# Attention with normalized queries and keys: half of the first shifted line of each batch made by GpSimd, squares made by VectorE

## The chip, the core and the metric

The kernel runs on one core of one Trainium2 chip. The metric is the device time of one execution in microseconds. A core has five engines that run side by side, each through its own list in its own order: TensorE (PE in the profile, its weight loads PEld), VectorE (DVE), ScalarE (ACT), GpSimd (POOL) and SyncE (SP, which issues DMAs). They wait for one another by semaphores.

## The reference

Attention of 32 heads, 2048 queries and keys, head size 20, all bf16. Queries and keys are divided by their norm, the logits are scaled by a number per head.

```python
qn = q / (jnp.sqrt((q * q).sum(axis=-1, keepdims=True)) + eps)
kn = k / (jnp.sqrt((k * k).sum(axis=-1, keepdims=True)) + eps)
logits = jnp.einsum('bhqd,bhkd->bhqk', qn, kn) * t[None, :, None, None]
attn = softmax(logits, axis=-1)
return jnp.einsum('bhqk,bhkd->bhqd', attn, v)
```

## The kernel before

**Tiling.** Four heads make a head group; there are eight. A head group has four query blocks of 512 queries (32 in all, numbered `sb`). A unit is 128 keys of one head against the 512 queries of a block: 64 units in a block. For each unit TensorE makes the logits in PSUM (128 keys by 512 queries), an engine turns them into exponentials in SBUF, and TensorE multiplies these with the values and adds into psO, one PSUM bank which belongs to one query block at a time. A column of ones beside the values gives the denominators.

**Two ways to the exponential.** In most units ScalarE does it, in waves of three and two units in turn (psA to pA, line 822; 14 waves fit in pA). The others, quota `ND_SB` = 18 of the 64 in a block and 20 in the last head group, go through VectorE: line 284 (`p1_op`, the conversion) multiplies a tile of psD and adds a constant so that the result, written as int16 and read as fp16, is about the exponential; `SHIFTS[0]` is part of the constant. Three more copies of it, shifted by the other numbers of `SHIFTS` (line 293, `chain_ops`: an int16 add), are multiplied with the values too, so that the errors of the four average out. One of the four copies is used a second time with values halved (`vhalf`): `COEF` says which, five products for each unit. Four units make a batch (`DB`): four conversions of 128x512, then three shift lines over the whole batch, 128x2048. Buffers dI, dS1, dS2, dS3 hold five batches (`NBD`); the batch number modulo five is the buffer number `bb`.

**Normalization.** For the next head group, while the current one is computed, `prep_ops` squares q and k (line 212 on GpSimd in pieces of 128x160, or line 216 on VectorE as 128x640), sums the squares (line 219), takes the inverse root on VectorE (lines 236 to 251) and scales (line 264, on GpSimd in pieces of two rows, `NM_ROWS`). DMAs transpose the result into qT and kT. The first head group does it all on VectorE. At the end of each query block VectorE transposes psO (line 315) and takes reciprocals (line 317), and GpSimd multiplies (line 319).

**Order.** All orders are fixed when the program is built. `make_plan` runs a small planner with assumed costs, step by step in time, and each engine gets its list from it. VectorE takes, of what is ready, the lowest priority number: 0 the end of a query block, 1 conversions (`PRIO1`), 1.5 normalization (`PRIO`), 2 shift lines. GpSimd's work lies in a list of its own with the same numbers (`step_pool`, line 956): it may start while VectorE is idle, or in the first 0.1 of an operation that the planner counts as free of the shared port (`port` false: the conversion, the transpose, sums, reciprocals; line 179). If it starts beside such an operation, it gets a wait on the VectorE operation before that one (lines 971 and 972), so that it starts with it on the chip too. VectorE operations with `port` true do not start in the planner while GpSimd is busy (line 941); on the chip no semaphore holds them. TensorE's list is made by `step_pe0`: logits when a PSUM buffer is free, else products with the values (`pv_round`, line 656), and only of the query block that owns psO; holes are filled with products of zeros (line 503).

Of the kernel before, what the change touches and what calls it, by code (L numbers as in the profile page):

```python
# [9 lines left out]
I32 = mybir.dt.int32  # L10
I16 = mybir.dt.int16
# [2 lines left out]
AXIS_X = mybir.AxisListType.X  # L14

LOG2E = 1.4426950408889634
SHIFTS = (382, 860, 565, 123)
COEF = ((1,), (1,), (1,), (1, .5))
LOG2K = 2.685380
NPV = sum(len(c) for c in COEF)  # L20

# [31 lines left out]
POOL2 = .0022  # L53
SQ_ROWS = 1
NM_ROWS = 2


class Op:
# [45 lines left out]
def bass_standalone__qk_norm__prompt_kernel(  # L104
# [7 lines left out]
    B, H, S, D = q.shape  # L112
# [5 lines left out]
    QW = 512  # L118

    with ExitStack() as es:  # L120
        sbuf = lambda name, shape, dt: es.enter_context(nc.sbuf_tensor(name, shape, dt))
# [19 lines left out]
        dI = sbuf("dI", [128, NBD, DB * QW], I16)  # L141
        dS = [dI] + [sbuf(f"dS{i}", [128, NBD, DB * QW], I16) for i in range(1, len(SHIFTS))]
        zt = sbuf("zt", [128, QW], BF16)
        iot = sbuf("iot", [128, 128], F32)
        idn = sbuf("idn", [128, 128], BF16)
        nr0 = sbuf("nr0", [128, 2, NH, 4], F32)
# [27 lines left out]
        def dve(name, n, rate, emit, reads, writes, ncols_fix=0.0, info=None):  # L174
            c = n * rate
            o = Op("DVE", name, emit, reads, writes, cost=0.069 + c + ncols_fix,
                   lat=0.135 + c + ncols_fix, info=info)

            o.port = name not in ("P1", "cp", "drain", "red", "inv", "rec")
            return o  # L180
# [7 lines left out]
        def prep_ops(hg, r0, r1, a0=0, a1=2, pool=False):  # L188
# [8 lines left out]
            for c0 in range(r0, r1, 4 * 2 // na):  # L197
                nn = min(4 * 2 // na, r1 - c0)
                bs = n_sq[0] % 2
                n_sq[0] += 1  # L200
                src = qk[b][:, a0:a1, :, c0:c0 + nn, :]
                w_ = na * NH * nn * D
                sq = sqs[bs][:, 0:w_]
                x3 = src.rearrange("p a h r d -> p (a h) (r d)")
                s3 = sq.rearrange("p (h x) -> p h x", h=na * NH)
                s4 = sq.rearrange("p (h r d) -> p h r d", h=na * NH, r=nn)
                o4 = ssum[b][:, a0:a1, :, c0:c0 + nn].rearrange("p a h r -> p (a h) r")
                if pool:
                    for c in range(0, nn, SQ_ROWS):
                        k0, k1 = c * D, min(c + SQ_ROWS, nn) * D  # L210
                        ops.append(pool_op("sq", na * NH * (k1 - k0), True,
                                           lambda e, o=s3[:, :, k0:k1], x=x3[:, :, k0:k1]: e.tensor_tensor(o, x, x, ALU.mult),  # L212
                                           kq, [("sqs", bs, c)]))
                else:
                    ops.append(dve("sq", w_, R2,
                                   lambda e, o=s3, x=x3: e.tensor_tensor(o, x, x, ALU.mult),
                                   kq, [("sqs", bs)] + [("sqs", bs, c) for c in range(R)]))
                ops.append(dve("red", w_, R1,
                               lambda e, o=o4, x=s4: e.tensor_reduce(o, x, AXIS_X, ALU.add),  # L219
                               [("sqs", bs)] + [("sqs", bs, c) for c in range(R)], [SS]))  # L220
# [59 lines left out]
        def p1_op(pb, bb, j):  # L280
# [3 lines left out]
                       lambda e: e.tensor_scalar(dst, psD[:, pb * QW:(pb + 1) * QW], 1024.0 * LOG2E, 15360.0 - 1024.0 * LOG2K + SHIFTS[0], ALU.mult, ALU.add),  # L284
                       [("psD", pb)], [("dI", bb, j)])

        def chain_ops(bb, nu):


            W = nu * QW  # L290
            kI = [("dI", bb, j) for j in range(nu)]
            return [dve(f"S{i}", W, R4,
                        lambda e, i=i: e.tensor_single_scalar(dS[i][:, bb, 0:W], dI[:, bb, 0:W],  # L293
                                                              float(SHIFTS[i] - SHIFTS[0]), ALU.add),
                        kI, [(f"dS{i}", bb, j) for j in range(nu)]) for i in range(1, len(SHIFTS))]

        def half_op(hg):
            b = hg % 2
# [78 lines left out]
        def make_plan(share):  # L377
# [57 lines left out]
            def finish(op, start, cost, lat):  # L435
                op.start, op.done = start, start + lat
                P.put(op)
# [9 lines left out]
            def zeros(i, after=()):  # L447
# [8 lines left out]
            finish(o, 0.05, o.cost, o.lat)  # L456
            o = P.link(Op("DVE", "z", lambda e: e.memset(act_scr[:, :], 1.0), [], ["scr"], 0.1, 0.15))
            finish(o, 0.3, o.cost, o.lat)
            o = P.link(dve("idn", 128, R1, lambda e: e.tensor_single_scalar(idn[:, :], iot[:, :], 0.0, ALU.is_equal),
                           ["iot"], ["idn"]))  # L460
            finish(o, 1.0, o.cost, o.lat)
# [403 lines left out]
            def step_qkd(used, with_a):  # L865
                nonlocal d_sb, issued_d
                while d_sb < NSB and d_left[d_sb] == 0:
                    d_sb += 1
                if d_sb >= NSB or d_sb > a_sb + 1:
                    return False  # L870
                if pe_mid:
                    return False
                rds = P.readers.get(("psD", issued_d % 2), [])
                if not all(r.done is not None and r.done + SEML <= now for r in rds):
                    return False
                if P.last_w.get(("psD", issued_d % 2)) is not None and not rds:
                    return False
                done_a = sum(quota[:a_sb]) + quota[a_sb] * (1 - a_left[a_sb] / aq[a_sb]) if a_sb < NSB else 1e9
                if issued_d > done_a + LEAD:
                    return False  # L880
                nb = len(batches)
                if batches and len(batches[-1]["u"]) < DB:
                    nb -= 1
                else:
                    if nb >= NBD:
                        old = [(nm, nb % NBD, j) for j in range(DB) for nm in ["dI"] + [f"dS{i}" for i in range(1, len(SHIFTS))]]
                        if any(x[3] in old for x in pending_pv):
                            return False
                if d_sb not in pool:
                    pool[d_sb] = units_of(d_sb)  # L890
                save = {hh: list(x) for hh, x in pool[d_sb].items()}
                us = take(d_sb, used, 1, "D")
                if not us or not keys_ready(us) or (with_a and us[0][1] in used):
                    pool[d_sb] = save
                    return False
                u = us[0]
                d_left[d_sb] -= 1
                pv_all[d_sb][u[1]] += NPV - 1
                pb = issued_d % 2
                issued_d += 1  # L900
                if not batches or len(batches[-1]["u"]) == DB:
                    batches.append({"u": [], "p": []})
                bt = batches[-1]
                bi = len(batches) - 1
                bb, j = bi % NBD, len(bt["u"])
                bt["u"].append(u)
                pe_group("QKD", [qk_mm(u, psD[:, pb * QW:(pb + 1) * QW])], "qk", qk_keys(u), [("psD", pb)], [u[1]])
                bt["p"].append(p1_op(pb, bb, j))
                want_dve(bt["p"][-1], PRIO1)
                total_left = sum(d_left)  # L910
                if len(bt["u"]) == DB or total_left == 0:
                    nu = len(bt["u"])
                    ch = chain_ops(bb, nu)
                    for o in ch:
                        want_dve(o, 2 + 0.001 * bi)
                    for j2, uu in enumerate(bt["u"]):
                        for i, cs in enumerate(COEF):
                            o, nm = (ch[i - 1], f"dS{i}") if i else (bt["p"][j2], "dI")
                            x = dS[i][:, bb, j2 * QW:(j2 + 1) * QW].bitcast(F16)
                            for c in cs:  # L920
                                pending_pv.append((o, uu, x, (nm, bb, j2), c != 1))
                return True
# [33 lines left out]
            def step_pool():  # L956

                on = P.order["DVE"]
                busy = free_["DVE"] > now
                if busy and (on[-1].port or now > on[-1].start + 0.1):  # L960
                    return False
                best = None
                for x in pool_todo:
                    ra_ = ready_at(x[2])
                    if ra_ is not None and ra_ <= now and (best is None or x[:2] < best[:2]):
                        best = x
                if best is None:
                    return False
                pool_todo.remove(best)
                o = best[2]  # L970
                if busy and len(on) > 1 and on[-2] not in o.deps:
                    o.deps.append(on[-2])
                finish(o, now, o.cost, o.lat)
                free_["POOL"] = now + o.cost
                return True
# [198 lines left out]
```

## Time and profile before

| | |
|---|---|
| runs, median (lowest to highest) | 720.33 us (720.0 to 721.35) |
| the profiled execution | 721.53 us |
| its span (first to last instruction) | 719.7 us |
| granted TensorE clock, mean | 0.994 |
| instructions | 17473 |
| ScalarE exponentials (L822) | 597 |
| VectorE conversions (L284), shift lines (L293) | 556, 417 |
| GpSimd squares (L212), scalings (L264), last products (L319) | 112, 112, 31 |

A row of the groups gives the line of the kernel, the engine, what is written and read with shapes and count, then the busy time in us, the mean of one in ns, and the idle time of the engine just before them with who ended it. A row of the timeline gives start, duration, engine, line and count; the same operations in a row are merged. Matmul ends are modelled, and a full TensorE may be full of zero products.

The chain of work that ended last runs by turns over TensorE (45%), ScalarE (37%) and VectorE (15%).

### The profile page before, as it was taken

To read this page: it belongs to the slowest core of one execution; us is meant where nothing else is said; L and a number is where in the kernel's file an instruction comes from. 1 tells how busy PE (TensorE), PEld (TensorE's weight loads), DVE (VectorE), ACT (ScalarE), POOL (GpSimd) and SP (SyncE) were. 2 spreads that over 40 slices of the span, in tenths; PEclk is the share of its full clock that TensorE was granted. 3 is DMA by queue.
4 is the path that set the end of the run, shared out by engine and by line. 5 is a ranking of instruction groups with operands and counts; after the bars stand their busy time and mean duration, and the time that the engine had idled before them with its cause. 6 is when DMAs were issued, how large, how long until landed. Compare 5 with 4: busy or idle time off the path is not lost.

```text
span 719.7 us, 17473 instructions
## 1 busy us (share of the span) xinstructions
PE 697.3 (97%) x7572; PEld 244.4 (34%) x7572; DVE 679.6 (94%) x1218; ACT 691.1 (96%) x605; POOL 135.1 (19%) x268
## 2 busy tenths in 40 slices
PE   7999999999999999999999999999999999999996
PEld 4433333433333333333333332342333433323332
DVE  6799959999999999999999999999999999999992
ACT  5999999979999999999999999999999989999996
POOL 2031234031040310311203130122201221000000
PEclk8999999999999999999999999999999999999999
DMA  5510133013030220300421022301203002000000
GB/s 60 83 7 2 30 68 38 2 30 68 1 39 1 31 66 2 37 2 1 82 29 26 1 45 53 38 2 31 67 1 38 1 18 44 2 19 7 1 6 14
DMA packets 113859, 19.68 MB, mean 27 GB/s; under 512 B 103024, under 2 KB 113776, under 8 KB 113776
## 3 DMA queue, kind: packets, MB, share of 16 engines
q1 hardware_dynamic: 112960, 18.37, 16.7%
q8 instruction: 61, 1.00, 0.6%
q10 hardware_dynamic: 816, 0.12, 0.1%
q14 instruction: 22, 0.18, 0.1%
HBM read 7.87 MB, written 2.62 MB: 15 GB/s over the span
## 4 chain that ended last, share of the span: by engine, by line
PE 45%; ACT 37%; DVE 15%; issue 0%; DMA 0%; ACTq 0%; SPq 0%
ACT pA L822 37%; PE psO L656 23%; PE psA L634 13%; DVE dS L293 7%; DVE dI L284 7%; PE psD L634 5%; PE psO L503 3%; DVE accT L315 1%; DVE ssum L219 1%; DMA tb<-in_t_dram 0%; ACTq L1121 0%; DVE vhalf L300 0%; DVE rsb L247 0%; DVE rsa L245 0%; DVE rsa L244 0%
## 5 line engine op out<-in xcount | busy, mean ns | idle before, releaser
L822 ACT ACTIVATE pA<-psA 128x1536 bf16<-128x1536 f32 x597 | 686.9, 1268 | 16.1 <-PE psD L634 9.9
L284 DVE TENSOR_SCALAR dI<-psD 128x512 int16<-128x512 f32 x556 | 355.5, 676 | 17.9 <-PE psD L634 15.5
L293 DVE TENSOR_SCALAR dS<-dI 128x2048 int16<-128x2048 int16 x417 | 276.0, 691 | 0.0
L634 PE MATMUL psA<-qT,kT 32*128 32x512 bf16 x1742 | 256.6, 384 | 7.7 <-ACT pA L822 4.5
L656 PE MATMUL psO<-dS,vaug 128*32 128x512 f16 x1668 | 222.5, 384 | 0.6 <-DVE dS L293 0.4
L656 PE MATMUL psO<-pA,vaug 128*32 128x512 bf16 x1492 | 221.0, 384 | 0.1
L634 PE MATMUL psD<-qT,kT 32*128 32x512 bf16 x556 | 178.9, 381 | 1.1 <-DVE dI L284 0.7
L634 PEld LDWEIGHTS psA<-qT,kT 32*128 32x128 bf16 x1742 | 62.9, 91 | 167.8 <-ACT pA L822 115.0
L656 PE MATMUL psO<-dI,vaug 128*32 128x512 f16 x556 | 115.3, 384 | 3.4 <-DVE accT L315 3.2
L656 PE MATMUL psO<-dS,vhalf 128*32 128x512 f16 x556 | 101.0, 382 | 0.3 <-DVE dS L293 0.2
L503 PE MATMUL psO<-zt 128*128 128x128 bf16 x976 | 101.0, 225 | 0.0
L319 POOL TENSOR_TENSOR ost<-accT,rec 128x320 bf16<-128x320 f32 x31 | 24.1, 777 | 354.2 <-DVE dS L293 246.4
L656 PEld LDWEIGHTS psO<-dS,vaug 128*32 128x32 bf16 x1668 | 60.1, 94 | 70.7 <-issue 33.8
L503 PEld LDWEIGHTS psO<-zt 128*128 128x128 bf16 x976 | 60.8, 99 | 66.2 <-issue 63.7
L656 PEld LDWEIGHTS psO<-pA,vaug 128*32 128x32 bf16 x1492 | 60.4, 94 | 56.1 <-issue 37.8
L212 POOL TENSOR_TENSOR sqs<-qk 128x160 bf16<-128x160 bf16 x112 | 50.8, 453 | 82.2 <-DVE dI L284 39.6
L634 PEld LDWEIGHTS psD<-qT,kT 32*128 32x128 bf16 x556 | 40.5, 91 | 50.1 <-DVE dI L284 29.0
L264 POOL TENSOR_TENSOR kpad<-qk,rn 128x160 bf16<-128x160 bf16 x56 | 26.3, 469 | 85.9 <-DVE dI L284 46.7
L656 PEld LDWEIGHTS psO<-dI,vaug 128*32 128x32 bf16 x556 | 30.0, 94 | 25.9 <-DVE accT L315 12.3
L264 POOL TENSOR_TENSOR qpad<-qk,rn 128x160 bf16<-128x160 bf16 x56 | 28.7, 517 | 42.6 <-DVE dS L293 36.0
L656 PEld LDWEIGHTS psO<-dS,vhalf 128*32 128x32 bf16 x556 | 26.3, 95 | 25.4 <-issue 13.5
L315 DVE STREAM_TRANSPOSE accT<-psO 128x512 f32<-128x512 f32 x32 | 22.6, 706 | 9.9 <-PE psO L656 9.9
(54 smaller groups left out, 101.3 us busy)
## 6 DMA issues: line engine op xcount, KB each, us to landing
vaug<-in_v_dram SPq DMA_DIRECT2D x32, 80.0 KB, 4.0
qk<-in_k_dram SPq DMA_DIRECT2D x7, 320.0 KB, 4.1
qk<-in_q_dram SPq DMA_DIRECT2D x7, 320.0 KB, 4.2
out_dram<-ost SPq DMA_DIRECT2D x28, 80.0 KB, 1.9
out_dram<-ost SPq DMA_DIRECT2D x14, 20.0 KB, 1.6
qk<-in_k_dram SPq DMA_DIRECT2D x1, 240.0 KB, 3.8
qk<-in_q_dram SPq DMA_DIRECT2D x1, 240.0 KB, 4.3
kT<-kpad SPq DMA_TRANSPOSE x8, 4.3
```

The source lines that it names most:

```text
L212: lambda e, o=s3[:, :, k0:k1], x=x3[:, :, k0:k1]: e.tensor_tensor(o, x, x, ALU.mult),
L219: lambda e, o=o4, x=s4: e.tensor_reduce(o, x, AXIS_X, ALU.add),
L264: emit = lambda e, o=dst, x=src, s=sc: e.tensor_tensor(o, x, s, ALU.mult)
L284: lambda e: e.tensor_scalar(dst, psD[:, pb * QW:(pb + 1) * QW], 1024.0 * LOG2E, 15360.0 - 1024.0 * LOG2K + SHIFTS[0], ALU.mult, ALU.add),
L293: lambda e, i=i: e.tensor_single_scalar(dS[i][:, bb, 0:W], dI[:, bb, 0:W], float(SHIFTS[i] - SHIFTS[0]), ALU.add),
L315: dve("drain", QW, R1, lambda e: e.transpose(aT[:, :, :].rearrange("p b d -> p (b d)"), psO[:, :]), ["psO"], [("accT", b)]),
L319: pool_op("omul", 320, True, lambda e: e.tensor_tensor(dst, num, rcb, ALU.mult), [("accT", b), ("rec", b)], [("ost", ob, qg)]) if pool else
L503: return lambda e: e.matmul(bank, zt[:, 0:128], zt[:, 0:n], start=False, stop=False, skip_group_check=True)
L634: return lambda e: e.matmul(dst, lhsT, rhs, tile_position=(32 * hh, 0))
L656: return lambda e: e.matmul(dst, lhsT, rhs, start=first, stop=last, skip_group_check=True, tile_position=(0, 32 * hh))
L822: a = Op("ACT", "exp", lambda e, s=src, d=dst: e.activation(d, s, ACT.Exp), [("psA", slot)], [("pA", pslot, i) for i in range(WAVES[slot]) ...
```

## The change

The first of the three shifted copies (number 1) is no longer made by VectorE for the whole batch. For the first two units of each batch GpSimd makes it, one operation for each unit, as soon as that unit's conversion is done; VectorE makes it for the other two units, 128x1024 in place of 128x2048. Copies 2 and 3 stay as they were. GpSimd's operation has one of two forms, by the buffer number: where `bb` is odd, pairs of int16 are added as int32 (256 elements, the second operand a constant column read with step 0); else 512 int16 elements get an immediate added. `SHIFTS` and `COEF` are turned by one place, so that the copy used twice is now dI itself, which the conversion makes. The squares of the later head groups are made by VectorE again. Shifts have priority 3 in GpSimd's list, and GpSimd may start in the first 0.3 of a conversion instead of 0.1; it does not start while VectorE is idle with something ready.

```diff
-SHIFTS = (382, 860, 565, 123)
-COEF = ((1,), (1,), (1,), (1, .5))
+SHIFTS = (123, 382, 860, 565)
+COEF = ((1, .5), (1,), (1,), (1,))
...
+SQ_POOL = False
+POOL_S = 1
+POOL_N = 2
+POOL_I32 = 2
+POOLPRIO = 3
+WIN = .3
...
+        shc = sbuf("shc", [128, len(SHIFTS)], I32)
...
-                if pool:
+                if pool and SQ_POOL:
...
+            for i in range(1, len(SHIFTS)):
+                j0 = POOL_N if i <= POOL_S else 0
...
+                sl = slice(j0 * QW, nu * QW)
+                ops.append(dve(f"S{i}", (nu - j0) * QW, R4,
+                               lambda e, i=i, sl=sl: e.tensor_single_scalar(dS[i][:, bb, sl], dI[:, bb, sl],
+                                                                            float(SHIFTS[i] - SHIFTS[0]), ALU.add),
...
+        def shift_op(i, bb, j):
+
+            sl = slice(j * QW, (j + 1) * QW)
+            o, x = dS[i][:, bb, sl], dI[:, bb, sl]
+            rd, wr = [("dI", bb, j), "shc"], [(f"dS{i}", bb, j)]
+            if POOL_I32 == 1 or POOL_I32 == 2 and bb % 2:
+                c = bass.AP(shc, shc[:, i:i + 1].offset, [shc[:, :].ap[0], [0, QW // 2]])
+                return pool_op(f"S{i}", QW // 2, True,
+                               lambda e: e.tensor_tensor(o.bitcast(I32), x.bitcast(I32), c, ALU.add), rd, wr)
+            return pool_op(f"S{i}", QW, False,
+                           lambda e: e.tensor_single_scalar(o, x, float(SHIFTS[i] - SHIFTS[0]), ALU.add), rd, wr)
...
+                    want_dve(Op("DVE", "z", lambda e, i=i: e.memset(shc[:, i:i + 1].bitcast(I16), SHIFTS[i] - SHIFTS[0]),
+                                [], ["shc"], 0.1, 0.15), 6)
...
+                for i in range(1, 1 + POOL_S):
+                    if j < POOL_N:
+                        made[i, bb, j] = shift_op(i, bb, j)
+                        want_dve(made[i, bb, j], POOLPRIO + 0.001 * bi)
...
-                if busy and (on[-1].port or now > on[-1].start + 0.1):
+                if busy and (on[-1].port or now > on[-1].start + WIN):
+                    return False
+                if not busy and any(ready_at(x[2]) is not None and ready_at(x[2]) <= now for x in dve_todo):
                     return False
```

More of the change, by code (lines that the diff above doesn't have):

```diff
@@ L285, in p1_op @@
                        [("psD", pb)], [("dI", bb, j)])
+        made = {}
         def chain_ops(bb, nu):
[L290 to L295, printed above, removed]
+            ops = []
+            for i in range(1, len(SHIFTS)):
+                j0 = POOL_N if i <= POOL_S else 0
+                if j0 >= nu:
+                    continue
+                sl = slice(j0 * QW, nu * QW)
+                ops.append(dve(f"S{i}", (nu - j0) * QW, R4,
+                               lambda e, i=i, sl=sl: e.tensor_single_scalar(dS[i][:, bb, sl], dI[:, bb, sl],
+                                                                            float(SHIFTS[i] - SHIFTS[0]), ALU.add),
+                               [("dI", bb, j) for j in range(j0, nu)], [(f"dS{i}", bb, j) for j in range(j0, nu)]))
+                for j in range(j0, nu):
+                    made[i, bb, j] = ops[-1]
+            return ops
+        def shift_op(i, bb, j):
[8 more added lines that the diff above has]
+                           lambda e: e.tensor_single_scalar(o, x, float(SHIFTS[i] - SHIFTS[0]), ALU.add), rd, wr)
         def half_op(hg):
@@ L458, in make_plan @@
             finish(o, 0.3, o.cost, o.lat)
+            if POOL_I32:
+                for i in range(1, 1 + POOL_S):
+                    want_dve(Op("DVE", "z", lambda e, i=i: e.memset(shc[:, i:i + 1].bitcast(I16), SHIFTS[i] - SHIFTS[0]),
+                                [], ["shc"], 0.1, 0.15), 6)
             o = P.link(dve("idn", 128, R1, lambda e: e.tensor_single_scalar(idn[:, :], iot[:, :], 0.0, ALU.is_equal),
@@ L909, in step_qkd @@
                 want_dve(bt["p"][-1], PRIO1)
+                for i in range(1, 1 + POOL_S):
+                    if j < POOL_N:
+                        made[i, bb, j] = shift_op(i, bb, j)
+                        want_dve(made[i, bb, j], POOLPRIO + 0.001 * bi)
                 total_left = sum(d_left)
@@ L917, in step_qkd @@
                         for i, cs in enumerate(COEF):
-                            o, nm = (ch[i - 1], f"dS{i}") if i else (bt["p"][j2], "dI")
+                            o = made[i, bb, j2] if i else bt["p"][j2]
+                            nm = f"dS{i}" if i else "dI"
                             x = dS[i][:, bb, j2 * QW:(j2 + 1) * QW].bitcast(F16)
```

## The prediction

> **What bounds the kernel now.** I read the busy shares first, then the busy time by stage, then ScalarE's own timeline for its gaps, then the groups of instructions, and last single stretches of VectorE and GpSimd side by side.
>
> ```profile
> PE 697.3 (97%) x7572; PEld 244.4 (34%) x7572; DVE 679.6 (94%) x1218; ACT 691.1 (96%) x605; POOL 135.1 (19%) x268
> ```
>
> Three engines are full, so averages decide nothing. By stage (columns: window, its length, then PE, PEld, DVE, ACT, POOL busy, clock, DMA):
>
> ```profile
> 95.00:150.00 55.00, 51.85 (x561) 20.72 (x553) 46.09 (x83) 48.17 (x43) 11.52 (x22) 1.00 0.22 35
> 150.00:310.00 160.00, 158.64 (x1736) 53.13 (x1728) 158.95 (x277) 159.44 (x139) 33.42 (x68) 1.00 0.20 31
> 310.00:580.00 270.00, 265.90 (x2946) 92.04 (x2949) 267.30 (x483) 265.71 (x232) 54.07 (x110) 1.00 0.17 28
> ```
>
> From 150 to 580 us VectorE (99%) and ScalarE (99%) are both saturated. TensorE is not: 101.0 us of its busy time are the zero matmuls of L503, which fill holes. The waits say who paces it: its loads for psA wait 115.0 us for ScalarE and its loads for psD 29.0 us for VectorE. ScalarE's work is fixed (597 exponentials, 686.9 us, the quotas are not touched), so I count where ScalarE stands still:
>
> ```profile
> 95.86 2.37 ACT L822 ACTIVATE pA<-psA 128x1536 bf16<-128x1536 f32 x2 [0.94 <-PE psA L634]
> 149.73 162.34 ACT L822 ACTIVATE pA<-psA 128x1536 bf16<-128x1536 f32 x140 [5.23 <-PE psD L634]
> 342.02 148.87 ACT L822 ACTIVATE pA<-psA 128x1024 bf16<-128x1024 f32 x129 [0.70 <-PE psD L634]
> 578.63 41.54 ACT L822 ACTIVATE pA<-psA 128x1536 bf16<-128x1536 f32 x36 [1.97 <-PE psD L634]
> 624.04 55.33 ACT L822 ACTIVATE pA<-psA 128x1536 bf16<-128x1536 f32 x48 [1.23 <-PE psD L634]
> ```
>
> The bracket is the idle time before. The span is 10.6 (to the first exponential) + 686.9 + 15.7 idle + 6.5 after the last. Of the 15.7, 3.4 lie before 100 us (ramp, first change of head group), 1.4 are crumbs under 0.2 us, and 10.9 lie from 149 us on. Those have one look: around 574 to 578 VectorE works off shifted lines and normalization, then the transpose at 574.94 frees psO, TensorE catches up with products and only at 578.19 serves psA. VectorE late, ScalarE starved. So 10.9 us (1.5%) is about all that a lighter VectorE can win; 12 with the crumbs.
>
> **The change, part by part.** Prices come from these groups (line, engine, out<-in, count | busy, mean ns):
>
> ```profile
> L284 DVE TENSOR_SCALAR dI<-psD 128x512 int16<-128x512 f32 x556 | 355.5, 676 | 17.9 <-PE psD L634 15.5
> L293 DVE TENSOR_SCALAR dS<-dI 128x2048 int16<-128x2048 int16 x417 | 276.0, 691 | 0.0
> L212 POOL TENSOR_TENSOR sqs<-qk 128x160 bf16<-128x160 bf16 x112 | 50.8, 453 | 82.2 <-DVE dI L284 39.6 <-DVE dS L293 29.5 <-DVE ssum L219 4.4
> L219 DVE TENSOR_REDUCE ssum<-sqs 128x32 f32<-128x640 bf16 x31 | 25.0, 806 | 0.0
> L216 DVE TENSOR_TENSOR sqs<-qk 128x640 bf16<-128x640 bf16 x3 | 1.5, 492 | 1.7 <-DMA qk<-in_q_dram 1.6
> L319 POOL TENSOR_TENSOR ost<-accT,rec 128x320 bf16<-128x320 f32 x31 | 24.1, 777 | 354.2 <-DVE dS L293 246.4
> L448 POOL MEMSET kpad<- 128x768 bf16 x2 | 1.5, 738 | 2.1 <-DVE flag L477 2.1
> L448 POOL MEMSET vaug<- 128x704 bf16 x2 | 1.4, 685 | 0.1
> ```
>
> *Taken from VectorE.* 417 / 3 = 139 batches; in each, one of three shift lines shrinks from 2048 to 1024 elements. Of the 0.68 us of a line some 0.17 is fixed (the reduce takes 806 ns for 640 elements and 486 for 320, so 1.0 ns a step and 0.17 besides), 0.51 is streaming; half of it is 0.26. 139 x 0.26 = 36 us off. Bounds: 0.22 to 0.30 a line, 31 to 42 us.
>
> *Given back to VectorE.* Seven head groups x 4 squares of 128x640. The row says 492 ns; back to back an instruction starts about 0.08 us before its forerunner's end (two conversions take 1.28, not 1.36), so a slot is 0.41: 28 x 0.41 = 11.5 us on.
>
> *GpSimd.* 112 squares (50.8 us) go, 278 shifts come. The form goes by buffer number, and with five buffers numbers 1 and 3 get int32: 56 batches, 112 operations of 256 int32 pairs; 83 batches give 166 operations of 512 int16 with an immediate. No row shows either. Two-input rows: 160 elements 453 ns, 320 elements 752 beside a conversion, so 1.87 ns an element and 0.15: the int32 form 0.63 us. For the immediate form the lower end is the memsets (0.83 ns an element and 0.10: 0.53 us), the upper the two-input slope (1.11 us). I take 0.56, near the memsets, because one operand is streamed in and not two. GpSimd's sum goes from 135 to 135 - 51 + 71 + 93 = 248 us, a third of the span.
>
> *What they cost VectorE.* The two engines exclude each other in some pairs:
>
> ```profile
> 162.00 1.22 DVE L284 TENSOR_SCALAR dI<-psD 128x512 int16<-128x512 f32 x2
> 163.14 0.87 DVE L293 TENSOR_SCALAR dS<-dI 128x2048 int16<-128x2048 int16 x1
> 162.71 0.75 POOL L319 TENSOR_TENSOR ost<-accT,rec 128x320 bf16<-128x320 f32 x1 [0.24 <-DVE dI L284]
> 91.92 3.55 DVE L293 TENSOR_SCALAR dS<-dI 128x2048 int16<-128x2048 int16 x4
> 92.28 3.50 POOL L264 TENSOR_TENSOR qpad<-qk,rn 128x160 bf16<-128x160 bf16 x4
> ```
>
> Beside conversions (L284) GpSimd and VectorE both run undisturbed. A GpSimd operation that outlasts its conversion holds the next shift line: begun at 162.71, 0.17 after the second conversion, it ends at 163.46, 0.32 after the shift line's start, and that line takes 0.87, which is 0.19 more. So 0.13 of overhang is free. Begun under shift lines, both suffer: four lines in 3.55 instead of 2.49 us, 0.27 each. A shift of length c, begun 0.16 behind a conversion of 0.60, delays the next line by c - 0.57: 0.06 for int32, nothing for the immediate form at 0.56. In VectorE's order 272 of 556 conversions are followed by another conversion, so 51% of the cases count: 112 x 0.51 x 0.06 = 3.4 us. At 1.11 the immediate form would add 166 x 0.51 x 0.54 = 46 us. The wider window (WIN .1 to .3) lets the other 143 operations end later; at most 0.09 x 143 x 0.51 = 6.6 us, I take 2.
>
> The Trainium skill ("SBUF — State Buffer", the part on ports) calls this an exclusive lock that a VectorE instruction in a two-port mode and a GpSimd instruction take in turn, whole instructions at a time, and "Perfetto Trace Analysis" (Optimizing Scalar/DVE Operations) warns that moving work between these two might not help; the pairs above bear out the lock. "GPSIMD Engine Reference" (section 3.1) gives 769 ns for a good loop over 512 elements, which would make the immediate form's price 85 x 0.20 = 17 us, an estimate.
>
> *Sum on VectorE*: -36 + 11.5 + 3.4 + 2 = -19 us, 2.7% of the span; bounds -30 and +36.
>
> *What is late next.* ScalarE. It can only win back its 10.9 us of late gaps. I take 8.5 of it (the four gaps over 0.6 us, 9.1, nearly all), less 1 for new waits of TensorE on shifts that come late: -7.5. The other edits cost nothing on the path: the reordered shifts change an immediate, and give dI two of five products, which are ready before any shift (in favour, unpriced); the added memset falls in the ramp, under 1.6 us of waiting for the first DMA. The new semaphore wait of a conversion on GpSimd's reading of an old buffer is covered by the ring of five batches, 5 x 4.96 = 25 us; without that cover the conversions stand behind it, and psD with them.
>
> From the profiled execution: 721.5 - 7.5 = 714.0 us (its span is 719.7). The runs' median is 720.33, 1.2 lower; I say **713.5**.
>
> **Rivals.**
>
> *GpSimd's queue lags (slower).* Of ready GpSimd work the planner takes normalization (priority 1.5) before shifts (3). From 342.5 to 351.5 us nearly every conversion already carries a scaling operation; 16 of them fill about 17 us. In that time 17 / 4.96 = 3.4 batches bring 7 shifts, which wait up to 17 us, and a query block's last product with them. ScalarE has 14 buffers of results ahead, 10 in 11.4 us, so 16 us. From there on it decides: a lag of 2 to 3 us beyond that, in each of 7 head groups, costs 14 to 21 and leaves 728 to 735 with the 7.5 won; a lag in half the groups leaves 722 to 725. Against it: where VectorE has nothing ready, GpSimd may run freely. Middle 727.
>
> *The lock eats it (slower).* The immediate form takes 1.0 us or more: 166 x 0.51 x 0.43 = 36 on VectorE, net +17, and as VectorE is saturated, 738. It turns at 0.80 us, or where 70 of the 278 shifts run beside shift lines (19 / 0.27). For it: no row shows the form. Against: the memsets' slope. This is what the warning of the Trainium skill would come to here.
>
> *The gaps are not VectorE's load.* They stem from the order at a change of query block; then ScalarE keeps its 15.7 us: 719 to 722, with the order shuffled a little either way.
>
> That the change does not do what it says is hardly open: the operations will show as POOL rows or not.
>
> **Numbers.** Forecast (709 to 719): 0.45. Gaps stay: 0.15. Queue lag: 0.25. Lock: 0.15. About 0.2% (1.4 us) is what measurement tells from no change. Faster: 0.45 and a third of the gaps case, 0.50; within 0.2%: 0.08; slower: the rest, 0.42. The range 709 to 731 leaves out the lock case, the worst lags and a few hundredths below. As both signs are likely: the forecast's own range is 709 to 719.
>
> **What will show it.** L293-like rows of 128x1024, 139 of them, near 0.42 us; 28 squares on DVE near 0.49; POOL rows near 0.63 (int32) and 0.56 (int16), and no shift lines stretched over 0.75 us but behind L319; VectorE below 97% busy from 150 to 580; ScalarE's late gaps under 4 us. Wrong if the immediate form is over 0.8 us, if TensorE's loads wait for POOL by more than 10 us in all, or if ScalarE's gaps stay with VectorE idle.

## The result, and the profile after

The changed kernel takes **756.51 us** (median of 4 runs, 752.24 to 761.13) against 720.63 before, 1.0499 times as long (95% interval 1.0432 to 1.0565). The forecast was 713.5, the range 709 to 731: wrong in sign and size. Ratios leave out executions over 1.5% above the fastest of their kernel, which run at a lower granted clock; all four of the changed kernel are in. The profiled execution took 758.14 us with a span of 756.3. The page's busy shares, clock row (40 slices) and main groups:

```profile
PE 716.1 (95%) x7501; PEld 244.5 (32%) x7501; DVE 688.7 (91%) x1247; ACT 697.5 (92%) x605; POOL 424.9 (56%) x434
...
PEclk9999979998999969999999999799999999999998
...
L854 ACT ACTIVATE pA<-psA 128x1536 bf16<-128x1536 f32 x597 | 693.2, 1256 | 45.1 <-PE psA L666 26.5
L291 DVE TENSOR_SCALAR dI<-psD 128x512 int16<-128x512 f32 x556 | 355.2, 678 | 31.5 <-PE psD L666 27.4
L323 POOL TENSOR_SCALAR dS<-dI 128x512 int16<-128x512 int16 x166 | 275.6, 1675 | 113.7 <-DVE dI L291 73.7
...
L688 PE MATMUL psO<-dS,vaug 128*32 128x512 f16 x1668 | 184.7, 387 | 11.9 <-POOL dS L323 10.9
```

The row of the exponentials before:

```profile
L822 ACT ACTIVATE pA<-psA 128x1536 bf16<-128x1536 f32 x597 | 686.9, 1268 | 16.1 <-PE psD L634 9.9
```

(L854 is the exponential, L291 the conversion, L306 the shift line, L321 and L323 GpSimd's shifts as int32 pairs and with an immediate.) One row stands out: the immediate form takes 1675 ns in the mean, not 560. GpSimd is busy 425 us and not 248. ScalarE stands idle 45.1 us before its exponentials instead of 16.1. And a digit that no step of the prediction looked at: the granted TensorE clock falls to 0.6 or 0.7 in single slices, 0.963 over the span against 0.994.

One stretch of the timeline shows all of it (VectorE, then GpSimd, then one row of TensorE and one of ScalarE):

```profile
162.79 1.87 DVE L291 TENSOR_SCALAR dI<-psD 128x512 int16<-128x512 f32 x3
164.58 1.00 DVE L306 TENSOR_SCALAR dS<-dI 128x2048 int16<-128x2048 int16 x1
165.51 1.27 DVE L291 TENSOR_SCALAR dI<-psD 128x512 int16<-128x512 f32 x2
166.70 3.12 DVE L306 TENSOR_SCALAR dS<-dI 128x2048 int16<-128x2048 int16 x4
172.88 0.69 DVE L291 TENSOR_SCALAR dI<-psD 128x512 int16<-128x512 f32 x1 [3.06 <-PE psD L666]
```

```profile
163.56 7.62 POOL L323 TENSOR_SCALAR dS<-dI 128x512 int16<-128x512 int16 x4
171.14 0.61 POOL L321 TENSOR_TENSOR dS<-dI,shc 128x256 int32<-128x256 int32 x1
```

```profile
171.22 0.61 PE L688 MATMUL psO<-dS,vaug 128*32 128x512 f16 x2 [2.87 <-POOL dS L323]
```

```profile
172.85 1.02 ACT L854 ACTIVATE pA<-psA 128x1024 bf16<-128x1024 f32 x1 [2.99 <-PE psD L666]
```

Four shifts in a row fill GpSimd for 7.62 us. VectorE's lines beside them take 1.00 us, and 3.12 for four. Then it backs up: TensorE stands 2.87 us before a product whose shift is still being made, VectorE 3.06 us and ScalarE 2.99 us behind TensorE. With the stall the clock falls (two windows of 10 us, and 5 us out of the second; PEclk is the third number from the end):

```profile
160.00:170.00 10.00, 7.48 (x89) 2.35 (x83) 9.83 (x16) 8.76 (x8) 8.84 (x8) 1.00 0.60 119
170.00:180.00 10.00, 8.78 (x72) 2.05 (x72) 4.84 (x8) 4.67 (x4) 7.00 (x8) 0.66 0.01 2
172.00:177.00 5.00, 5.00 (x43) 1.17 (x43) 2.22 (x4) 2.38 (x3) 2.25 (x3) 0.50 0.01 3
```

From 170 to 180 us VectorE and ScalarE are half idle behind TensorE. Its 0.66 is a mean: from 172 to 177 us the clock is 0.50, and from 178 us on it is whole again.

### The profile page after: what moved, and what is told of

Read it like the earlier page. It is cut to its first block, busy times and chain, and to the rows that moved or that the text cites. A ratio compares the mean times of both kernels' runs of the same rounds, so it can differ in the third digit from the quotient of the medians.

```text
span 756.3 us, 17533 instructions
## 1 busy us (share of the span) xinstructions
PE 716.1 (95%) x7501; PEld 244.5 (32%) x7501; DVE 688.7 (91%) x1247; ACT 697.5 (92%) x605; POOL 424.9 (56%) x434
## 3 DMA queue, kind: packets, MB, share of 16 engines
q1 hardware_dynamic: 112960, 18.37, 16.1%
## 4 chain that ended last, share of the span: by engine, by line
DVE 42%; PE 35%; ACT 17%; POOL 4%; issue 1%; DMA 0%; ACTq 0%; SPq 0%; DVEq 0%
DVE dI L291 22%; DVE dS L306 17%; ACT pA L854 17%; PE psO L688 17%; PE psA L666 10%; PE psD L666 4%; POOL dS L323 4%; PE psO L535 4%; DVE accT L343 1%; DMA tb<-in_t_dram 0%; DVE vhalf L328 0%; POOL dS L321 0%; DVE rec L345 0%; DVE rn L282 0%; DVE rn L258 0%
## 5 line engine op out<-in xcount | busy, mean ns | idle before, releaser
L854 ACT ACTIVATE pA<-psA 128x1536 bf16<-128x1536 f32 x597 | 693.2, 1256 | 45.1 <-PE psA L666 26.5
L291 DVE TENSOR_SCALAR dI<-psD 128x512 int16<-128x512 f32 x556 | 355.2, 678 | 31.5 <-PE psD L666 27.4
L323 POOL TENSOR_SCALAR dS<-dI 128x512 int16<-128x512 int16 x166 | 275.6, 1675 | 113.7 <-DVE dI L291 73.7
L666 PE MATMUL psA<-qT,kT 32*128 32x512 bf16 x1782 | 270.7, 394 | 8.5 <-ACT pA L854 6.1
L306 DVE TENSOR_SCALAR dS<-dI 128x2048 int16<-128x2048 int16 (+1 forms) x417 | 265.9, 668 | 0.1
L688 PE MATMUL psO<-dS,vaug 128*32 128x512 f16 x1668 | 184.7, 387 | 11.9 <-POOL dS L323 10.9
L688 PE MATMUL psO<-pA,vaug 128*32 128x512 bf16 x1492 | 189.9, 400 | 0.2 <-ACT pA L854 0.2
L321 POOL TENSOR_TENSOR dS<-dI,shc 128x256 int32<-128x256 int32 x112 | 70.0, 637 | 39.2 <-DVE dI L291 24.2
L688 PE MATMUL psO<-dI,vaug 128*32 128x512 f16 x556 | 82.4, 385 | 4.1 <-DVE accT L343 4.0
L688 PE MATMUL psO<-dI,vhalf 128*32 128x512 f16 x556 | 84.6, 384 | 0.0
L688 PEld LDWEIGHTS psO<-dS,vaug 128*32 128x32 bf16 x1668 | 51.1, 95 | 90.3 <-issue 37.1
L688 PEld LDWEIGHTS psO<-pA,vaug 128*32 128x32 bf16 x1492 | 50.0, 95 | 59.5 <-issue 45.9
L271 POOL TENSOR_TENSOR kpad<-qk,rn 128x160 bf16<-128x160 bf16 x56 | 26.2, 469 | 37.5 <-DVE dS L306 28.5
```

Of the source, the lines that this page charges most:

```text
L271: emit = lambda e, o=dst, x=src, s=sc: e.tensor_tensor(o, x, s, ALU.mult)
L306: lambda e, i=i, sl=sl: e.tensor_single_scalar(dS[i][:, bb, sl], dI[:, bb, sl], float(SHIFTS[i] - SHIFTS[0]), ALU.add),
L321: lambda e: e.tensor_tensor(o.bitcast(I32), x.bitcast(I32), c, ALU.add), rd, wr)
L323: lambda e: e.tensor_single_scalar(o, x, float(SHIFTS[i] - SHIFTS[0]), ALU.add), rd, wr)
L666: return lambda e: e.matmul(dst, lhsT, rhs, tile_position=(32 * hh, 0))
L688: return lambda e: e.matmul(dst, lhsT, rhs, start=first, stop=last, skip_group_check=True, tile_position=(0, 32 * hh))
```

## The experiments

Theory A: the immediate form is the cause, because it is long. Rival B: GpSimd's queue lags whatever the form. Rival C: the gaps are not VectorE's load, or the squares (or the turned order) cost the time. Kernels are variants of the changed one unless said otherwise; the kernel before measured 721 to 722 us beside them.

**All shifts as int32 pairs.**

```diff
-POOL_I32 = 2
+POOL_I32 = 1
```

> The changed kernel with all 278 GpSimd shifts as int32 pairs (0.64 us each by the row of the changed kernel), none with an immediate. Theory A (the immediate form is the cause: 1.49 us undisturbed instead of 0.56, so it outlasts its conversion, stretches the shift lines by the lock and makes TensorE wait): the sum of the prediction holds with its middle values, 711 to 717 us, shift lines over 0.75 us only a few, granted clock back at 0.99. Theory B (GpSimd's queue lags behind normalization, whatever the form): 722 to 733 us, with TensorE's loads waiting for POOL as in the changed kernel. Theory C (the gaps are not VectorE's load, or the squares eat the gain): 718 to 723 us.

Measured 715.24 us, ratio 0.9909 (0.9884 to 0.9935), clock 0.995. One number of the program turns +5.0% into -0.9%. Its groups by shape:

```profile
L306 DVE TENSOR_SCALAR dS<-dI 128x2048 int16<-128x2048 int16 x278 | 189.5, 695 | 0.0
L306 DVE TENSOR_SCALAR dS<-dI 128x1024 int16<-128x1024 int16 x139 | 59.7, 429 | 0.1
```

and from its page:

```profile
L854 ACT ACTIVATE pA<-psA 128x1536 bf16<-128x1536 f32 x597 | 689.1, 1263 | 8.1 <-PE psA L666 4.4
...
L321 POOL TENSOR_TENSOR dS<-dI,shc 128x256 int32<-128x256 int32 x278 | 169.3, 614 | 286.4 <-DVE dI L291 175.7
```

A half line costs 0.27 us less than a whole one, the int32 form 0.61 us, and ScalarE's idle time falls from 16.1 to 8.1. Theory A holds, B and C do not for this form.

**All shifts with the immediate.** `POOL_I32 = 0`.

> The changed kernel with all 278 shifts in the immediate form. Theory A: the loss grows with the number of such operations, 166 to 278: of about 43 us between all-int32 (714) and the mix (757) by the same share, 714 + 43 x 278 / 166 = 786 us or more, as GpSimd is then busy some 278 x 1.65 + 80 = 540 us and lags; clock under 0.96. Theories B and C: within 1% of the mix, 750 to 764 us.

Measured 782.25, 797.22, 797.94 and 801.12 us, at clocks of 0.949, 0.923, 0.922 and 0.915. A said 786 or more, which the fastest misses by 4 us, and a clock under 0.96. GpSimd is busy 532.6 us in the profiled execution (797.94 us). The loss grows with the count: with 0, 166 and 278 such operations the fastest executions take 714, 752 and 782 us.

**No shift on GpSimd.** `POOL_N = 0`: squares on VectorE, turned order and wider window are left.

> The changed kernel with no shift on GpSimd (all three shift lines over the whole batch on VectorE), so what is left of the change is the squares on VectorE, the turned order of the shifts and the wider window. VectorE gets 11.5 us more than before. Theory A: VectorE saturated, so up to that, 722 to 732 us. Theory C (squares or the turned order are what costs): over 740 us.

Measured 729.44 us, 1.0139 (1.0084 to 1.0193): 8.4 us for VectorE's 11.5 more, as A said. The clock of the profiled execution is 0.995, and its shift lines are:

```profile
L306 DVE TENSOR_SCALAR dS<-dI 128x2048 int16<-128x2048 int16 x417 | 276.4, 690 | 0.0
```

Against it the int32 shifts win 14.2 us.

**The planner told the true price.**

```diff
-POOL1 = .0009
+POOL1 = .00268
```

> The changed kernel with the planner's price of the immediate form raised from 0.58 to 1.49 us (POOL1), so that the order is made for what the chip does; the operations are the same. If the loss lies in the length itself (VectorE held by the lock): 745 to 765 us. If it lies in the order made for a wrong price (TensorE standing before products whose shifts are late, and its clock falling): 722 to 735 us and a clock of 0.98 or more.

Measured 742.66 us, 1.029 (1.0263 to 1.0316), clock 0.991: between the two ranges, so neither branch came true as it stood. The operations are the same, so 13.9 us of the loss come from the order made for the wrong price; the other 27 to all-int32 do not come back. Waits for GpSimd's shifts (us in total, times, longest), first in the changed kernel:

```profile
PEld psO L688 <- POOL dS L323: 17.9, 18, 3.2
...
PE psO L688 <- POOL dS L323: 10.9, 12, 2.9
```

and with the true price:

```profile
POOL dS L323 <- DVE dS L306: 93.2, 61, 4.9
...
PEld psO L688 <- POOL dS L323: 1.9, 6, 0.4
```

With the waits for int32 shifts, the loads waited 20.7 us and the products 11.4 more in the changed kernel; here the loads wait 3.1. The shift lines became shorter too: both lengths together take 261.1 us, where they take 274.8 in the changed kernel and 249.2 in all-int32. So the new order mends waits and stretched lines at once. Of the 27 us that stay, 11.9 are stretched lines; where the other 15 arise, no run shows.

**The lock alone.** VectorE makes all shift lines; the 166 immediate operations stay at their places but write to a spare buffer.

```diff
...
-                j0 = POOL_N if i <= POOL_S else 0
+                j0 = 0
...
-            o, x = dS[i][:, bb, sl], dI[:, bb, sl]
+            o, x = idle[:, (2 * (bb // 2 % 2) + j) * QW:(2 * (bb // 2 % 2) + j + 1) * QW], dI[:, bb, sl]
...
-                    if j < POOL_N:
-                        made[i, bb, j] = shift_op(i, bb, j)
+                    if j < POOL_N and not bb % 2:
+                        want_dve(shift_op(i, bb, j), POOLPRIO + 0.001 * bi)
```

> The kernel with no shift on GpSimd (729.4 us) plus the 166 immediate operations of the changed kernel at their places, written to a spare buffer that nothing reads; VectorE makes all shift lines, TensorE never waits for GpSimd's shifts. If the loss is VectorE being held by the lock (the stretched lines of the changed kernel come to some 31 us more than their plain length): 750 to 762 us, VectorE's lines over 0.75 us as many as there. If it is TensorE standing before late shifts: 729 to 738 us.

Measured 753.23 us (1.0445, 1.0376 to 1.0514), 23.8 over its base of 729.44. The profile (line 308 is the shift line here):

```profile
L308 DVE TENSOR_SCALAR dS<-dI 128x2048 int16<-128x2048 int16 x417 | 302.6, 752 | 0.0
```

302.6 against 276.4 us: 26.2 us of stretched lines, which covers the 23.8, with no product waiting for these operations and the clock of the profiled execution at 0.994. The time lies in the range for the lock. So VectorE being held is enough for about 24 us. In the changed kernel the lines are stretched by as much (274.8 against 249.2 us in all-int32); if that costs as much there, some 17 of the 41.3 us between these two are left for late shifts and the clock. This is an estimate: the 13.9 us that the true price brought back are no proof of it, as they came with shorter lines too.

**More zero products**, to hold the clock.

```diff
-HEAT = .57
+HEAT = .80
```

> The changed kernel with more zero products in TensorE's holes (HEAT .57 to .80), nothing else. If a part of the loss is the granted clock, which falls where TensorE stands before a late shift (0.50 to 0.68 in some stretches of 10 us), the clock comes back to 0.98 or more and the time falls to 735 to 747 us. If the clock is only a sign of the waiting: 752 to 762 us with the clock up. If zero products get in the way of logits: over 765.

Measured 758.9 us, clock 0.965. No branch came true: zero products went from 865 to 1106 and the clock hardly rose (0.963 to 0.978 over four executions, against 0.957 to 0.970), so this run does not tell. They stand in TensorE's list, so none runs while the list stands before a late shift; that this is the reason is not shown. How much of the 17 us is waiting and how much the clock stays open. The four runs of the changed kernel give a hint only: 752.24, 754.89, 758.14 and 761.13 us at clocks of 0.970, 0.964, 0.963 and 0.957.

**Seven forms on GpSimd, by themselves**, added to the kernel before, on a constant tile, written to a buffer that nothing reads.

```diff
...
+                        lambda e, d=d: e.tensor_single_scalar(d[0], z16, 259.0, ALU.add),
+                        lambda e, d=d: e.tensor_single_scalar(d[1][:, 0:256], z16[:, 0:256], 259.0, ALU.add),
+                        lambda e, d=d: e.tensor_tensor(d[2].bitcast(I32), z16.bitcast(I32), col, ALU.add),
+                        lambda e, d=d: e.tensor_tensor(d[3].bitcast(BF16), zt[:, :], zt[:, :], ALU.add),
+                        lambda e, d=d: e.tensor_single_scalar(d[4].bitcast(BF16), zt[:, :], 0.5, ALU.mult),
+                        lambda e, d=d: e.tensor_copy(d[5], z16),
+                        lambda e, d=d: e.tensor_single_scalar(d[6].bitcast(F32), z16.bitcast(F32), 0.5, ALU.mult))):
...
```

> The kernel before with fourteen extra GpSimd operations on a constant tile early in the run, each of seven forms twice, written to a spare buffer that nothing reads. Shortest durations count. If the int16 type makes the immediate form dear (conversion of each element): 512 int16 with an immediate 1.49 us, 256 of them 0.78, a copy of 512 int16 dear too (over 1 us), but 512 bf16 with an immediate 0.5 to 1.1 us. If the immediate form as such is dear: bf16 with an immediate also near 1.49. int32 pairs with a constant column 0.61. The sums of the run mean nothing.

The whole kernel took 733.73 us in its one execution, which is not used. Minimum, median and maximum of two each, in ns:

```profile
L495 POOL TENSOR_SCALAR pscr<-zt x2: 1489/1654/1818, 8.3 to 15.3; 128x512 int16<-128x512 int16 x2
L496 POOL TENSOR_SCALAR pscr<-zt x2: 842/874/907, 10.1 to 16.8; 128x256 int16<-128x256 int16 x2
L497 POOL TENSOR_TENSOR pscr<-zt,pcol x2: 606/666/725, 10.9 to 17.7; 128x256 int32<-128x256 int32 x2
L498 POOL TENSOR_TENSOR pscr<-zt x2: 1032/1032/1032, 11.5 to 18.4; 128x512 bf16<-128x512 bf16 x2
L499 POOL TENSOR_SCALAR pscr<-zt x2: 1487/1609/1731, 12.5 to 19.4; 128x512 bf16<-128x512 bf16 x2
L500 POOL COPY pscr<-zt x2: 605/615/625, 13.9 to 21.1; 128x512 int16<-128x512 int16 x2
L501 POOL TENSOR_SCALAR pscr<-zt x2: 843/843/843, 14.5 to 21.6; 128x256 f32<-128x256 f32 x2
```

The type is innocent (int16, bf16: 1489, 1487; int16, f32 at 256: 842, 843), and so is the arithmetic, a sum for int16 and a product for the other two. The form as such is dear: (1489 - 842) / 256 = 2.5 ns an element and 0.2 us besides, while a plain copy of 512 takes 0.61 and a sum of two tensors 1.03. My idea of a conversion of int16 fell.

**Squares back on GpSimd, all int32.** `SQ_POOL = True`, `POOL_I32 = 1`.

> All shifts as int32 pairs, and the squares back on GpSimd (undoes that part of the change). VectorE is spared 11.5 us more, GpSimd gets 112 operations of 0.45 us more in the stretches where it is fullest. If VectorE's load still sets ScalarE's gaps (8 us of them left with int32 alone): 709 to 713 us. If GpSimd's queue lags once it is fuller (the second rival): 717 to 727 us. If ScalarE is the only limit left: 713 to 717.

Measured 714.68 us, 0.9888 (0.9823 to 0.9952): the same as with squares on VectorE. It lies in the range where ScalarE is the only limit left, though ScalarE still stands idle 8.8 us; 11.5 us less for VectorE no longer shorten its gaps. GpSimd's 304 us of work do not lag (rival B).

**The turned order alone**, in the kernel before.

> The kernel before with only the turned order of the shifts and products (dI used twice, in place of the last shifted copy). By the prediction it costs nothing on the path and may help a little, as two of five products are ready before any shift: 714 to 721 us. If the turned order is what made all-int32 faster and not the shifts: 715 to 717.

Measured 718.79 us, 0.9985 (0.9944 to 1.0026): no difference that shows, as predicted. It did not make all-int32 faster by itself.

**The narrow window, all int32.** `WIN = .1`.

> All shifts as int32 pairs (715.2 us) with the planner's start window for GpSimd back at 0.1 of a conversion (WIN). The prediction took 2 us for the wider window. Fewer overhangs with 0.1, but fewer places: 712 to 716 if the window costs its 2 us, 718 to 728 if without it GpSimd's queue lags (second rival).

Measured 721.8 us, 0.998 (0.9942 to 1.0018), in the second range; ScalarE's idle time is 17.2 us against 8.1 (in an execution of 725.32 us). The wide window, which I priced at 2 us of cost, earns some 5 us by the two ratios and 6.6 by the medians. TensorE's loads wait only 2.9 us for GpSimd's shifts on the chip, so late shifts are not it. I read it as rival B's effect inside the planner, shifts placed later because there are fewer places, which no run here shows by itself.

**One more unit in 64 for VectorE, all int32**: `ND_SB = 19`, `ND_SB_LAST = 21`, first with squares on VectorE, then on GpSimd.

> All shifts as int32 pairs and one more unit in 64 from ScalarE to VectorE (ND_SB 19, in the last head group 21). ScalarE loses 32 units of about 0.46 us, 14 us; VectorE gets 32 x (0.60 + (2 x 0.60 + 0.34) / 4) = 31 us, and has some 33 us idle between 20 and 700 us. If ScalarE is now the limit: 701 to 708 us; if VectorE is full: 714 to 725.

> The same with the squares on GpSimd, which spares VectorE 11.5 us. If ScalarE is the limit: 700 to 706 us, as VectorE is still not full; if GpSimd's fuller queue lags: 708 to 720.

Measured 742.98 us (1.0321, 1.024 to 1.0402) and 736.71 us (1.018, 1.0105 to 1.0255): both misses. ScalarE's work falls to 674.3 us, but it stands idle 47.8. These two numbers are of the first. VectorE is busy 695.7 of 740.4 us in the first and 685.9 of 741.8 in the second (an execution of 743.91 us, the longest of its four), so its busy share does not single it out; a unit moved to VectorE also gives TensorE five products for one. Which of the two limits here was not separated. All-int32 with the quotas as they are is the best version measured, 0.9% to 1.1% below the kernel before.

## Why the prediction was wrong

- *What bounds the kernel* (VectorE late, ScalarE starved, about 10.9 us to be won): right. With int32 ScalarE's idle time falls by 8.0 us and the time by 5.8 (721.08 to 715.24), where the sum had 7.5. One reading was loose: the 101.0 us of zero products belong to the whole span; between 150 and 580 us they take 54.2.
- *Taken from VectorE*, 0.26 us a line: right, 695 - 429 = 0.27. *Given back*, 11.5 us of squares: 488 ns each after; 8.4 us of time alone.
- *The int32 form*, 0.63 us: right, 0.61.
- ***The immediate form, "I take 0.56, near the memsets, because one operand is streamed in and not two": the step that failed.*** 1.49 us undisturbed, outside even my bounds of 0.53 to 1.11. A memset has no input; its row was near in name only. And the upper bound assumed that one operand can't cost more than two; it can. With int32 at these 166 places, the time is 715.24 and not 756.51 us.
- *The price to VectorE*: the overhang rule was right in kind, and the place where it turns, 0.80 us, was named. At 1.49 us the rule gives 166 x 0.51 x 0.92 = 78 us, where the lock alone showed 26 us of stretched lines: a long operation also covers the next conversions, and many end under a conversion again (77 of the 166 in that run's trace). The lock rival had the mechanism with a chance of 0.15, its price (738) taken at 1.0 us. The rule of "SBUF — State Buffer" in the Trainium skill, that the two engines exclude each other whole instructions at a time, agrees in kind: VectorE's lines grow from 276.4 to 302.6 us. The estimate from "GPSIMD Engine Reference" (section 3.1, 769 ns) does not: 1489 ns measured for 512 elements.
- *What is late next* ("less 1 for new waits of TensorE"): wrong with the long form: 32.1 us of loads and products waiting for GpSimd's shifts, and a clock of 0.963, which no case had. Two of the signs that the prediction named for being wrong came: the form over 0.8 us, and loads waiting for POOL by more than 10 us (20.7).
- *Rivals*: the queue lag did not come with int32 (715.2 and 714.7); it is one reading, not shown, of the loss with the narrow window. That the gaps are not VectorE's load fell with all-int32.
- *The window*: priced at 2 us against, measured 5 to 7 in favour. Without it all-int32 gains nothing (721.8), so that all-int32 came near the forecast is in part luck.

## What to carry to other kernels

Price an operation that the trace doesn't show by measuring that form; a row of another operation, however near it looks, is no bound, and one unmeasured form at 166 places was the whole difference between 0.9% faster and 5% slower. Work for GpSimd fits beside VectorE as long as each operation ends inside a VectorE operation that leaves it free (here 0.61 us under conversions of 0.60); past that it holds VectorE wherever a shift line is next and, in a fixed order, everything that was planned behind it. If the planner's prices are wrong, its order adds a loss of its own (here 14 of 41 us, which the true price brings back).

## What the runs showed of the hardware that I had not expected

On GpSimd an operation with an immediate is slower than one on two tensors: 512 elements of bf16 take 1.49 us with an immediate and 1.03 as a sum of two tensors; a copy of 512 int16 takes 0.61.

The granted clock has two values in the changed kernel, 1.00 and 0.50. In the profiled execution it falls to 0.50 at 102.8, 171.1, 270.0, 369.0 and 478.3 us, for 13.7, 6.8, 13.7, 3.4 and 10.2 us, 48 us in all; all-int32 shows 1.00 from 20 to 700 us. Only the fall at 171.1 us comes with a long stall, the 2.87 us above; its 6.8 us at half the clock are worth 3.4, more than the stall itself. In the 7 us before each of the other four, TensorE never stands over 1.2 us at a time. Before the first, several short waits leave it busy for 1.98 of 3.40 us:

```profile
99.40:102.80 3.40, 1.98 (x26) 0.50 (x24) 2.83 (x5) 2.95 (x3) 3.40 (x3) 1.00 0.00 0
103.00:116.00 13.00, 13.00 (x81) 4.17 (x80) 9.39 (x15) 8.28 (x7) 8.60 (x8) 0.50 0.13 9
```

Before the last the busy time shows no hole at all; what made the clock fall there stays open. Extra zero products in TensorE's list did not prevent it (clock 0.965 with 1106 of them, 0.963 with 865, in the profiled executions). The Trainium skill states a rule which I had not weighed: "TensorE: Matmul & The Clock Gate" (Why this matters for your kernels) asks for no idle gaps over some 3 us between matmuls, or the clock goes back to half. The 0.50 agrees, and the 2.87 us come near the 3; the other four falls had no such gap.
